# Attention and FFN in one kernel: softmax denominators spread by DMA, a projection bank shared, and 28 more score units on VectorE

## The chip, the cores and the metric

The kernel runs on one core of a Trainium2 chip. The metric is device time in microseconds (us) of one execution; the time before is 755.69 us, the median of three runs (754.64 to 756.87). Engines: TensorE (PE; its weight loads are PEld), VectorE (DVE), ScalarE (ACT), GpSimd (POOL) and SyncE (SP), whose queue issues nearly all DMAs.

## The reference

S = 2048 rows, D = 640, H = 32 query heads of Dh = 20 that share one key and one value head, F = 1536. All inputs are bf16.

```python
def _A_ref(x, wq, wk, wv, wo):
    q = (x @ wq).reshape(B, S, H, Dh).transpose(0, 2, 1, 3)
    k = x @ wk
    v = x @ wv
    scores = jnp.einsum("bhqd,bkd->bhqk", q, k) * (Dh ** -0.5)
    p = _softmax(scores, axis=-1)
    o = jnp.einsum("bhqk,bkd->bhqd", p, v)
    return o.transpose(0, 2, 1, 3).reshape(B, S, H * Dh) @ wo
def _B_ref(x, w1, b1, w2, b2):
    h = jnp.einsum("bsd,df->bsf", x, w1) + b1
    r = jnp.where(h > 0, h, 0)
    return jnp.einsum("bsf,fd->bsd", r * r, w2) + b2
xn = _layernorm(x, axis=-1)
return x + _A_ref(xn, A_wq, A_wk, A_wv, A_wo) + _B_ref(xn, B_w1, B_b1, B_w2, B_b2)
```

## The kernel before

**Blocks, tiles, units.** The queries are cut into 4 chunks of 512 rows and the heads into 8 groups of 4, which makes 32 blocks. A block needs the scores of its 4 heads against 16 tiles of 128 keys; a *unit* is one head against one tile (128 keys x 512 queries, one PSUM bank). Four units of a tile make one group of value products (PV), whose four heads stand in rows 0, 32, 64 and 96 of one PSUM bank. In the value operand, column 20 holds ones, so row 32h + 20 of the result is the softmax denominator of head h.

**Two ways to an exponential.** Most units go to ScalarE, which reads two or three banks at once and writes exp into `PT` (L790, `S_EXP`). The `QUOTA` list says how many of each block's 16 tiles go to VectorE instead: `[1, 3] + [4, 3, 4] * 9 + [4, 4, 4]`, 115 tiles or 460 units. There one instruction per unit turns scores into integers (`S_P1`, L875, result in `T8`), and four instructions per tile (`S_PH`, L901, result in `PB`) make four shifted copies whose bits are read as bf16 and whose weighted sum, made by four groups of PV products instead of one, approximates the exponential. A VectorE tile therefore costs four L875, four L901 and four PV groups.

**Banks.** Banks 0 to 2 and 3 to 5 are the two triples for scores. The third bank of each triple (2 is `XD`, 5 is `DB`) holds either the third unit of an exponential or one unit for VectorE. Bank 6 is `PVB` (the PV sum) and bank 7 `MB`, in which projections of queries, FFN rows and outputs (L521) are made one after the other (`S_MISC`).

**Who sets the order.** The program has a planner: while it is built, generators (`S_QK`, `S_D`, `S_PV`, `norm` and others) ask for instructions with modelled durations, and `Sched.run` writes one fixed list per engine from them. Each engine then executes its list in that order and waits on semaphores where a result is not there. `pos()` is the place in the ScalarE units, in blocks; `gates` say from which position a VectorE tile may start; the `U(at, ...)` list gives the position from which a projection may start. The planner counts 60 ns for an SP issue and a fixed landing time for each DMA. Requests marked `under` are GpSimd instructions that are put beneath a VectorE instruction that reads PSUM (`beneath`), after the last VectorE instruction marked `port`.

**Normalization.** When a block's PV sum is complete, `norm` transposes it out of PSUM in 32 x 32 squares (L987), which brings the denominators into columns, takes reciprocals of 128 x 16 values (L991), multiplies in two halves on GpSimd (L993) and transposes back into `OTn` (L1013), the operand of the output projection. The outputs of a chunk (`u_OUT`, L521 and L642) follow once its eight blocks are normalized; those of the last chunk are made in two parts, the first (`u_P1`) during the last blocks, the rest after the end of the scores. `out_tail` adds the residual from `x_sb`, which has stayed in SBUF since the start, and stores with a DMA on SP (L647).

**FFN.** `u_FFN` makes 12 rows of the hidden layer per chunk (L607), which GpSimd squares (L617); the `U` list spaces them half a block apart.

Of the kernel before, what the change touches and what calls it, by code (L numbers as in the profile page):

```python
# [14 lines left out]
HPG = 4  # L15
# [25 lines left out]
QUOTA = [1, 3] + [4, 3, 4] * 9 + [4, 4, 4]  # L41
RING = 20
NT8 = 3
NPB = 5
NQS = 4
EVP = 1
DLEAD = 0.45
DWAIT = 120.0
DALONE = 1500.0
DBEHIND = (1.5, 0.0)  # L50
QLATE = 0.15
PG, PAT = 4, 28.4

SEM_NS = 60.0
PE_WIN = 3420.0
PE_MISC = 9000.0
# [28 lines left out]
class Req:  # L85


    def __init__(self, alts, deps, prio, name="", mode=None, deadline=None, rows=None, after=0.0, cols=0.0, even=False, port=False, under=False):
        self.alts = alts if isinstance(alts, list) else [alts]
        self.deps, self.prio, self.name, self.mode = deps, prio, name, mode  # L90
        self.deadline, self.rows, self.after = deadline, rows, after
        self.cols, self.even, self.port, self.under = cols, even, port, under
# [7 lines left out]
class Sched:  # L100
# [17 lines left out]

    def room(self, t, c):
        tot = self.load(t) + c  # L120
        for s_, c_ in self.win:
            if tot <= PE_MISC:
                break
            if s_ > t - PE_WIN:
                tot -= c_
                t2 = s_ + PE_WIN
                t = max(t, t2)
        return t
# [19 lines left out]
    def run(self):  # L148
        while self.streams:
# [7 lines left out]
            cands = []  # L157
            for st in self.streams:
# [7 lines left out]
                if deps is None or rr.under:  # L166
                    continue
                t0 = max([d.done + SEM_NS for d in deps] + [rr.after])
                best = None
                for k, (eng, dur, lat, ins) in enumerate(rr.alts):  # L170
# [3 lines left out]
                    if rr.even:  # L174
                        est = self.room(est, rr.cols)
# [4 lines left out]
                cands.append((best[1], best[2], rr, deps, best[3], best[4], st))  # L180
            if not cands:
                raise RuntimeError("stuck at %.0f: %s" % (self.now, [s[2] for s in self.streams]))
# [70 lines left out]
    def resolve(self, newsem):  # L253
# [37 lines left out]
        for e in self.ENG:  # L291
            n = 0
            for op in self.lists[e]:
                if op.dma is not None:
                    op.sig, op.sem, op.amt, op.val = True, newsem("d_" + op.dma), 16, 16
                elif op.sig:
                    n += 1
                    op.sem, op.amt, op.val = sems[e], 1, n

    def emit(self, eng, e):  # L300
        for op in self.lists[eng]:
# [7 lines left out]
            for f in op.ins:  # L309
                ins = f(e)  # L310
            if op.sig and op.ins:
# [6 lines left out]
def bass_parallel_sum__grouped_kv_mqa__dense_activation_squared_relu__prompt_kernel(nc, A_x, A_wq, A_wk, A_wv, A_wo, B_x, B_w1, B_b1, B_w2, B_b2, out):  # L318
    es = ExitStack()
    with es:  # L320
# [3 lines left out]
        x_sb = sb("x_sb", [128, ST, D], BF16)  # L324
# [21 lines left out]
        PB = sb("PB", [128, NPB, HPG, 512], I16)  # L346
        Tn = sb("Tn", [128, 2, 512], F32)
        rd = sb("rd", [128, 2, 16], F32)
        T2 = sb("T2", [128, 2, 512], BF16)
# [37 lines left out]
        def dma(eng, name, fn, deps, land):  # L387
            def gen():
                op = yield Req((eng, 60.0 if eng == "sp" else 500.0, land, [fn]), deps, 0, name)
# [134 lines left out]
        def groups(gl, n, b_, deps, p, name, m=32, gdeps=None):  # L524
            v = None
            for k, (L, R) in enumerate(gl):
# [3 lines left out]
                elif gdeps is not None:  # L530
                    dd = dd + gdeps[k]
                v = yield Req(("pe", PE512 if n > 400 else PE320, (PE512 if n > 400 else PE320) + PELAT, col4(L, R, n, b_, k == 0, k == len(gl) - 1, m)),
                              dd, p, name, mode="col", cols=512.0 if n > 400 else 320.0, even=p >= 3)
# [89 lines left out]
        olast = {}  # L623

# [14 lines left out]
        def out_tail(v, st, hh, in1, b_, extra=()):  # L639
# [5 lines left out]
            olast[(st, hh)] = w  # L645
            if (st, 1 - hh) in olast:
# [8 lines left out]
        def u_OUT(qc, st, hh, b_):  # L655
# [7 lines left out]
            yield from out_tail(v, st, hh, x_sb[:, st, cs], b_)  # L663

        def u_P1(st, hh, gs, b_):
# [5 lines left out]
            v = yield Req(("dve", 450.0, 491.0, [lambda e: e.tensor_tensor(out=part[:, st % 4, cs], in0=ps[:, b_, 0:320], in1=x_sb[:, st, cs], op=ALU.add)]), [v], EVP, f"PE1_{st}_{hh}")  # L671
            done[f"PP{st}_{hh}"] = v
            bank[b_].last = [v]
# [7 lines left out]
        def u_FULL(st, hh, b_):  # L681
# [4 lines left out]
            yield from out_tail(v, st, hh, x_sb[:, st, cs], b_)  # L686
# [51 lines left out]
        def S_QK():  # L738
            k = 0
            slot = 0  # L740
            while apos[0] < len(aunits):
# [4 lines left out]
                n = 2 if busy[b3] or ("DBfree" if b3 == DB else "XDfree") not in done or d_behind() > DBEHIND[k % 2] else 3  # L746
# [64 lines left out]
        mbusy = [0]  # L811
        gates = [b + m / float(QUOTA[b]) - DLEAD for b, m, t in dtiles] + [float(NBLK)]

        def d_behind():
            p = pos()
            want = sum(4.0 * min(1.0, max(0.0, (p - gates[n]) / (gates[n + 1] - gates[n]))) for n in range(len(dtiles)))
            return want - nd[0]
        phq = []

        def S_D():  # L820
            todo = list(enumerate(dtiles))
            opened = []
            while todo or opened:
# [10 lines left out]
                def poll():  # L834
                    fb = [x for x in (DB, XD) if not busy[x] and (open3[x] or "QKend" in done) and bank[x].last is not None]
                    if not fb:
# [48 lines left out]

        def S_PH():
            for want in range(len(dtiles)):
# [5 lines left out]
                op = None  # L893
                for j in range(NPH):
                    k = (n * NPH + j) % NPB

                    def deps():
                        if pbres[k].last is None:
                            return None
                        return [acc[-1]] + pbres[k].last  # L900
                    op = yield Req(("dve", 600.0, 640.0, [lambda e, j=j, k=k, s=s: e.tensor_scalar(out=PB[:, k, :, :], in0=T8[:, s, :, :], scalar1=PH_D[j], scalar2=0.5,  # L901
                                                                                             op0=ALU.add, op1=ALU.mult)]), deps, 4, "PH", port=True)
                    pbres[k].last = None
                    pv_items[b].append(("D", t, (j, k), op))
                t8res[s].last = [op]
# [5 lines left out]
        def S_FILL():  # L911
# [4 lines left out]
            while "QKend" not in done:  # L916
                def poll():
# [7 lines left out]
                    if not pv_open[0]:  # L925
                        fb = [x for x in (MB, DB) if not (busy[DB] or not open3[DB] if x == DB else mbusy[0]) and "DBfree" in done and max(o.done for o in bank[x].last) + SEM_NS <= t + 40.0]
# [57 lines left out]
        def norm(b, pv):  # L984
            qc, g = divmod(b, G)
            a = b % 2
            v = yield Req(("dve", 700.0, 717.0, [lambda e: e.transpose(out=Tn[:, a, :], in_=ps[:, PVB, :])]), (lambda: get(*([f"NB{b - 2}"] if b >= 2 else [])) and [pv] + get(f"NB{b - 2}") if b >= 2 else [pv]), 0, f"N1_{b}")  # L987
            bank[PVB].last = [v]
            if b == NBLK - 1:
                done["PVend"] = True  # L990
            w = yield Req(("dve", 160.0, 234.0, [lambda e: e.reciprocal(out=rd[:, a, :], in_=Tn[:, a, DH:512:32])]), [v], 1.5, f"N2_{b}")  # L991
            def n3(e, c0, c1):
                return e.tensor_tensor(out=T2[:, a, 32 * c0:32 * c1].rearrange("p (c d) -> p c d", d=32), in0=Tn[:, a, 32 * c0:32 * c1].rearrange("p (c d) -> p c d", d=32),  # L993
                                       in1=rd[:, a, c0:c1].rearrange("p (c o) -> p c o", o=1).to_broadcast([128, c1 - c0, 32]), op=ALU.mult)
            if b == NBLK - 1:
                w = yield Req(("dve", 650.0, 688.0, [lambda e: n3(e, 0, 16)]), [w], 1.5, f"N3_{b}", port=True)
            else:
                r = w
                w = yield Req(("pool", 540.0, 600.0, [lambda e: n3(e, 0, 8)]), [r], 0, f"N3_{b}", under=True)
                w = yield Req(("pool", 540.0, 600.0, [lambda e: n3(e, 8, 16)]), [r], 0, f"N3_{b}", under=True)  # L1000

            def deps():
                dd = [w]
                if b < 2:
                    dd += done["junk"]
                if qc >= 2:
                    names = [f"O{qc - 2}_{st}_{hh}" for st in range(4 * qc - 8, 4 * qc - 4) for hh in range(2)]
                    o = get(*names)
                    if o is None:
                        return None  # L1010
                    dd += o
                return dd
            w = yield Req(("dve", 690.0, 707.0, [lambda e: e.transpose(out=OTn[:, qc % 2, g, :], in_=T2[:, a, :])]), deps, 1.5, f"N4_{b}")  # L1013
# [165 lines left out]
```

## Time and profile before

| | us |
|---|---|
| median of three runs | 755.69 |
| the profiled execution's own time | 755.73 |
| its span, first to last instruction | 753.9 |
| first exponential starts / last ends | 16.2 / 743.5 |
| TensorE's granted clock over the run | 0.998 of full |

The span is made of a ramp of about 25 us in which x is loaded, normalized and transposed, a long stretch of scores, and a tail from 743.5 us on with the last block's normalization and the last projections. The waits of VectorE's instructions:

```profile
DVE T L875 <- PE ps L728: 23.0, 30, 2.4
DVE hT_tmp L607 <- PE ps L521: 3.8, 4, 1.9
DVE w_sb L671 <- PE ps L521: 3.2, 2, 1.9
DVE qT L579 <- PE ps L521: 2.0, 2, 1.8
```

Each line names the waiting instruction and what it waited for, then the total in us, the number of times and the longest wait. A long total is only of weight where the engine that waits is needed at that time.

### The profile page before, as it was taken

How to read it: one execution, taken by the hardware profiler on the slowest of the kernel's cores; microseconds unless marked ns; L12 is line 12 of the kernel's file. 1: busy time of each engine (PE TensorE's matmuls, PEld its weight loads, DVE VectorE, ACT ScalarE, POOL GpSimd, SP SyncE). 2: the span in 40 equal slices, each digit the busy share in tenths (PEclk: the TensorE clock that was granted, in tenths of full speed). 3: DMA queues.
4: the chain of work that ended last, by engine and by line, in shares of the span. 5: the costliest groups of instructions: out<-in, count | busy, mean ns of one | idle time of the engine just before them, and what ended most of it. 6: DMA issues, size and time to landing. Idle time of an engine off the chain costs nothing.

```text
span 753.9 us, 22837 instructions
## 1 busy us (share of the span) xinstructions
PE 725.3 (96%) x10243; PEld 234.6 (31%) x10243; DVE 702.5 (93%) x1222; ACT 734.0 (97%) x756; POOL 113.1 (15%) x200
## 2 busy tenths in 40 slices
PE   8999999999999999999999999999999999999996
PEld 3422222222233333332223333333223333333333
DVE  6789999999998998999999989989999998899995
ACT  5999999999999999999999999999999999999994
POOL 4321111111011111012221001101222100000000
PEclk9999999999999999999999999999999999999999
DMA  8600000000000000000000000000000000000001
GB/s 257 184 2 1 2 2 2 1 2 2 1 3 10 2 10 2 10 2 10 2 2 3 10 3 10 2 10 10 2 2 2 5 7 11 11 11 2 3 2 37
DMA packets 9412, 12.33 MB, mean 16 GB/s; under 512 B 1761, under 2 KB 8674, under 8 KB 9314
## 3 DMA queue, kind: packets, MB, share of 16 engines
q1 hardware_dynamic: 8002, 10.82, 4.5%
q8 instruction: 80, 1.31, 0.8%
q10 hardware_dynamic: 1312, 0.05, 0.1%
q14 instruction: 18, 0.15, 0.1%
HBM read 8.25 MB, written 2.62 MB: 14 GB/s over the span
## 4 chain that ended last, share of the span: by engine, by line
ACT 84%; PE 15%; DVE 1%; issue 0%; POOL 0%; DVEq 0%; POOLq 0%
ACT PT L790 84%; PE ps L521 4%; PE ps L967 4%; PE ps L728 4%; PE ps L440 1%; DVE out_sb L642 0%; PE ps L915 0%; DVE kT L545 0%; PE ps L510 0%; DVE Tn L987 0%; DVE OTn L1013 0%; DVE T L993 0%; DVE xnT L505 0%; POOL hT_tmp L422 0%; DVEq L320 0%
## 5 line engine op out<-in xcount | busy, mean ns | idle before, releaser
L790 ACT ACTIVATE PT<-ps 128x1024 bf16<-128x1024 f32 (+2 forms) x733 | 725.8, 1182 | 1.6 <-PE ps L728 1.5
L875 DVE TENSOR_SCALAR T<-ps 128x512 uint16<-128x512 f32 x460 | 302.9, 678 | 24.1 <-PE ps L728 23.0
L728 PE MATMUL ps<-qT,kT 20*128 20x512 bf16 x2048 | 287.6, 384 | 19.9 <-ACT PT L790 16.2
L901 DVE TENSOR_SCALAR PB<-T 128x2048 int16<-128x2048 uint16 x460 | 299.8, 685 | 0.9
L967 PE MATMUL ps<-PB,vp 128*32 128x512 bf16 x1840 | 166.7, 382 | 1.1 <-DVE PB L901 0.6
L728 PEld LDWEIGHTS ps<-qT,kT 20*128 20x128 bf16 x2048 | 71.3, 91 | 283.4 <-ACT PT L790 271.7
L967 PE MATMUL ps<-PT,vx 128*32 128x512 bf16 x1588 | 157.7, 389 | 0.0
L617 POOL TENSOR_TENSOR big<-hT_tmp 128x256 bf16<-128x256 bf16 x96 | 58.4, 614 | 306.4 <-DVE PB L901 154.7
L521 PE MATMUL ps<-w_sb,big 128*32 128x320 bf16 x1536 | 85.2, 301 | 0.0
L993 POOL TENSOR_TENSOR T<-Tn,rd 128x256 bf16<-128x256 f32 x62 | 37.9, 617 | 285.5 <-DVE PB L901 212.8
L521 PE MATMUL ps<-xnT,w_sb 128*32 128x512 bf16 x960 | 77.7, 382 | 0.3 <-DVE out_sb L642 0.2
L967 PEld LDWEIGHTS ps<-PT,vx 128*32 128x32 bf16 x1588 | 40.5, 93 | 82.8 <-issue 81.5
L967 PEld LDWEIGHTS ps<-PB,vp 128*32 128x32 bf16 x1840 | 44.8, 95 | 45.3 <-issue 16.3
L521 PE MATMUL ps<-wo_pad,OTn 128*32 128x320 bf16 x1024 | 54.2, 301 | 0.8 <-DVE OTn L1013 0.8
L521 PE MATMUL ps<-xnT,wq_sb 128*20 128x512 bf16 x640 | 51.2, 380 | 0.0
L521 PEld LDWEIGHTS ps<-w_sb,big 128*32 128x32 bf16 x1536 | 36.7, 96 | 28.1 <-issue 15.4
L607 DVE TENSOR_SCALAR hT_tmp<-ps,b1col 128x512 bf16<-128x512 f32 x48 | 35.5, 739 | 4.3 <-PE ps L521 3.8
L521 PEld LDWEIGHTS ps<-wo_pad,OTn 128*32 128x32 bf16 x1024 | 24.6, 96 | 18.5 <-issue 7.4
L521 PEld LDWEIGHTS ps<-xnT,w_sb 128*32 128x32 bf16 x960 | 21.8, 95 | 22.0 <-issue 10.6
L912 PE MATMUL ps<-kT,zeros 128*32 128x512 bf16 x276 | 24.9, 381 | 0.0
L987 DVE STREAM_TRANSPOSE Tn<-ps 128x512 f32<-128x512 f32 x32 | 22.7, 710 | 1.0 <-PE ps L967 0.9
L579 DVE TENSOR_SCALAR qT<-ps 128x512 bf16<-128x512 f32 x31 | 21.2, 685 | 2.5 <-PE ps L521 2.0
(56 smaller groups left out, 169.7 us busy)
## 6 DMA issues: line engine op xcount, KB each, us to landing
w_sb<-in_B_w_dram SPq DMA_DIRECT2D x2, 1920.0 KB, 11.8
out_dram<-out_sb SPq DMA_DIRECT2D x16, 160.0 KB, 1.8
x_sb<-in_A_x_dram SPq DMA_DIRECT2D x3, 640.0 KB, 8.9
wq_sb<-in_A_wq_dram SPq DMA_DIRECT2D x1, 800.0 KB, 6.4
wo_pad<-in_A_wo_dram SPq DMA_DIRECT2D x4, 200.0 KB
x_sb<-in_A_x_dram SPq DMA_DIRECT2D x2, 320.0 KB, 4.0
wk_c<-in_A_wk_dram ACTq DMA_DIRECT2D x1, 25.0 KB, 3.8
wv_c<-in_A_wv_dram ACTq DMA_DIRECT2D x1, 25.0 KB, 4.6
```

Of the source, the lines that this page charges most:

```text
L521: return lambda e: e.matmul(ps[32 * j:32 * j + m, b_, 0:n], Lj, R, start=first, stop=last, tile_position=(0, 32 * j))
L579: alts = [("dve", 620.0, 660.0, [lambda e: e.tensor_scalar(out=dst, in0=ps[:, b_, :], scalar1=QSCALE, scalar2=None, op0=ALU.mult)])]
L607: v = yield Req(("dve", 690.0, 750.0, [lambda e: e.tensor_scalar(out=hT_tmp[:, k, :], in0=ps[:, b_, :], scalar1=b1col[:, f:f + 1], scalar2 ...
L617: w = yield Req(("pool", 540.0, 600.0, [lambda e, hs=hs: e.tensor_tensor(out=h2T[:, qc % 2, f, hs], in0=hT_tmp[:, k, hs], in1=hT_tmp[:, k, ...
L728: ins.append(lambda e, i=i, b=b, t=t, h=h: e.matmul(ps[:, b0 + i, :], kT[32 * h:32 * h + DH, t * 128:(t + 1) * 128], qT[32 * h:32 * h + DH ...
L790: op = yield Req(("act", d_, d_ + 100.0, [lambda e, slot=slot, n=n, b0=b0: e.activation(out=PT[:, slot:slot + n, :], in_=ps[:, b0:b0 + n, ...
L875: op = yield Req(("dve", 600.0, 660.0, [lambda e, s=s, h=h, bk=bk: e.tensor_scalar(out=T8[:, s, h, :], in0=ps[:, bk, :], scalar1=OFFS, sca ...
L901: op = yield Req(("dve", 600.0, 640.0, [lambda e, j=j, k=k, s=s: e.tensor_scalar(out=PB[:, k, :, :], in0=T8[:, s, :, :], scalar1=PH_D[j], ...
L912: fill = [(lambda e, h=h: e.matmul(ps[32 * h:32 * h + 32, PVB, :], zeros32[:, :], kT[:, 0:512], start=False, stop=False, tile_position=(0, ...
L967: ins = [(lambda e, h=h, first=first, last=last: e.matmul(ps[32 * h:32 * h + 32, PVB, :], lhs, rhs[h], start=first, stop=last, tile_positi ...
L987: v = yield Req(("dve", 700.0, 717.0, [lambda e: e.transpose(out=Tn[:, a, :], in_=ps[:, PVB, :])]), (lambda: get(*([f"NB{b - 2}"] if b >= ...
L993: return e.tensor_tensor(out=T2[:, a, 32 * c0:32 * c1].rearrange("p (c d) -> p c d", d=32), in0=Tn[:, a, 32 * c0:32 * c1].rearrange("p (c ...
```

## The change

1. **Quota.** `[1, 3] + [4] * 29 + [2]`: 122 tiles, 488 units on VectorE, 1560 on ScalarE. `T8` has four buffers instead of three and `PB` six instead of five; `PB` takes the next free buffer instead of a fixed one.
2. **Denominators.** Except for the last block, both transposes go. A copy brings the PV sum to SBUF; four DMAs spread the four denominator rows over 32 partitions each, VectorE takes the reciprocals, four DMAs bring them back into rows, and four DMAs broadcast each row over its head's 32 partitions. GpSimd multiplies, straight into `OTn`. The last block keeps the old way (`norm_last`).
3. **Banks.** VectorE units may also use the projection bank `MB` while no projection is due and at most two units are open; the choice between two and three units for an exponential follows whether a VectorE unit is due and none is in flight.
4. **FFN rows.** They may start from block 0.8, 4.0, 12.2 and 20.2 for the four chunks, 0.2 blocks apart.
5. **Space.** `PB` lies where `x_sb` was; the residual is loaded again from DRAM, 16 DMAs of one row tile each into `xres`.
6. **The planner.** `under` requests may also be placed while VectorE is free for their length; the pacing of projections (`even`, `room`) goes. An option to share L901's work with GpSimd is added and off (`SHARE = False`).

```diff
-QUOTA = [1, 3] + [4, 3, 4] * 9 + [4, 4, 4]
+QUOTA = [1,3]+[4]*29+[2]
-NT8 = 3
-NPB = 5
+NT8 = 4
+NPB = 6
+SHARE = False
-DBEHIND = (1.5, 0.0)
+FAT = (0.8, 4.0, 12.2, 20.2)
+FSTEP = 0.2
+MBD = 2
+MBSLACK = .02
+MBEND = 30.0
+GIVE = 2
+OUTM = (1,1)
...
+                if rr.under:
+                    eng, dur, lat, ins = rr.alts[0]
+                    est = max(self.free[eng], t0, self.port, self.free["dve"])
+                    below.append((est, dur, rr, deps + ([self.last_port] if self.last_port is not None else []), 0, eng, st))
+                    continue
...
+            idle = min([c[0] for c in cands if c[5] == "dve"] + [1e12])
+            cands += [c for c in below if c[0] + c[1] <= idle + 50.0]
...
-        x_sb = sb("x_sb", [128, ST, D], BF16)
+        pbx = sb("pbx", [128, NPB * HPG * 512], I16)
+        PB = pbx[:, :].rearrange("p (k h n) -> p k h n", k=NPB, h=HPG)
+        x_sb = pbx[:, 0:ST * D].bitcast(BF16).rearrange("p (st d) -> p st d", st=ST)
+        xres = sb("xres", [128, 4, D], BF16)
...
+        def x_again(st):
+            yield Until(lambda: pos() >= min(8 * (st // 4) + 7.0, PAT - 1.0) and (st < 4 or ((st - 4, 0) in xuse and (st - 4, 1) in xuse)))
+            dma("sp", f"xr{st}", lambda e: e.dma_start(xres[:, st % 4, :], xv[:, st, :]), [xuse[(st - 4, hh)] for hh in range(2)] if st >= 4 else [], 2500.0)
...
-                n = 2 if busy[b3] or ("DBfree" if b3 == DB else "XDfree") not in done or d_behind() > DBEHIND[k % 2] else 3
+                n = 2 if busy[b3] or ("DBfree" if b3 == DB else "XDfree") not in done or wants() and nd[0] - nd[1] < OUTM[k % 2] else 3
...
-                    if not fb:
+                    if not busy[MB] and not mbusy[0] and misc_slack() and nd[0] - nd[1] < MBD:
+                        fb.append(MB)
+                    if not fb or nd[0] - nd[1] >= GIVE:
                         return None
...
-            w = yield Req(("dve", 690.0, 707.0, [lambda e: e.transpose(out=OTn[:, qc % 2, g, :], in_=T2[:, a, :])]), deps, 1.5, f"N4_{b}")
+            v = yield Req(("dve", 640.0, 700.0, [lambda e: e.tensor_copy(out=Tn[:, a, :], in_=ps[:, PVB, :])]), (lambda: None if old() is None else [pv] + old()), 0, f"N1_{b}")
+            bank[PVB].last = [v]
+            dma("sp", f"da{b}", [(lambda e, h=h: e.dma_start(dn[32 * h:32 * h + 32, a, :], Tn[32 * h + DH:32 * h + DH + 1, a, :].rearrange("p (r c) -> p r c", c=16))) for h in range(HPG)], [v], 2300.0)
+            yield Until(lambda: have(f"da{b}"))
+            w = yield Req(("dve", 90.0, 160.0, [lambda e: e.reciprocal(out=rd[:, a, :], in_=dn[:, a, :])]), [done[f"da{b}"]], 1.5, f"N2_{b}")
+            dma("sp", f"db{b}", [(lambda e, h=h: e.dma_start(Rr[32 * h:32 * h + 1, :].rearrange("p (r c) -> p r c", c=16), rd[32 * h:32 * h + 32, a, :])) for h in range(HPG)],
+                [w] + ([] if b < 1 else [done[f"dc{b - 1}"]]), 2300.0)
+            yield Until(lambda: have(f"db{b}"))
+            dma("sp", f"dc{b}", [(lambda e, h=h: e.dma_start(Rb[32 * h:32 * h + 32, a, :], Rr[32 * h:32 * h + 1, :].rearrange("p (o n) -> p o n", o=1).to_broadcast([1, 32, 512]))) for h in range(HPG)],
+                [done[f"db{b}"]] + old(), 2600.0)
+            yield Until(lambda: have(f"dc{b}"))
+            w = []
+            for i in range(2):
+                c = slice(256 * i, 256 * i + 256)
+                w.append((yield Req(("pool", 540.0, 600.0, [lambda e, c=c: e.tensor_tensor(out=OTn[:, qc % 2, g, c], in0=Tn[:, a, c], in1=Rb[:, a, c], op=ALU.mult)]),
+                                    (lambda: None if free() is None else [done[f"dc{b}"]] + free()), 0, f"N3_{b}", under=True)))
+            done[f"NB{b}"] = w[-1]
...
-                at = 1.0 + (FT * qc + f) * 0.5
+                at = FAT[qc] + f * FSTEP
```

## The prediction

> **What bounds the kernel now.** I read the engines' busy shares first, then the chain that ended last, then the busy times of the stretch between the ramp and the tail (25 to 735 us), then who waited for whom, and last the timeline of ScalarE and VectorE.
>
> ```profile
> PE 725.3 (96%) x10243; PEld 234.6 (31%) x10243; DVE 702.5 (93%) x1222; ACT 734.0 (97%) x756; POOL 113.1 (15%) x200
> ACT 84%; PE 15%; DVE 1%; issue 0%; POOL 0%; DVEq 0%; POOLq 0%
> ```
> ```profile
> 25.00:735.00 710.00, 690.67 (x9739) 218.27 (x9731) 673.47 (x1143) 709.30 (x720) 103.41 (x173) 1.00 0.02 6
> ```
> The numbers after the length are PE, PEld, DVE, ACT and POOL. ScalarE is busy in 709.3 of 710 us: its exponentials (L790) set the pace. VectorE follows with 673.5, 95%; it has 36.5 us left.
>
> ```profile
> L790 ACT ACTIVATE PT<-ps 128x1024 bf16<-128x1024 f32 x609 | 583.1, 1110 | 1.6 <-PE ps L728 1.5
> L875 DVE TENSOR_SCALAR T<-ps 128x512 uint16<-128x512 f32 x460 | 302.9, 678 | 24.1 <-PE ps L728 23.0
> L901 DVE TENSOR_SCALAR PB<-T 128x2048 int16<-128x2048 uint16 x460 | 299.8, 685 | 0.9
> L790 ACT ACTIVATE PT<-ps 128x1536 bf16<-128x1536 f32 x123 | 187.6, 1542 | 0.0
> L987 DVE STREAM_TRANSPOSE Tn<-ps 128x512 f32<-128x512 f32 x32 | 22.7, 710 | 1.0 <-PE ps L967 0.9
> L1013 DVE STREAM_TRANSPOSE OTn<-T 128x512 bf16<-128x512 bf16 x32 | 22.5, 702 | 0.2
> L993 POOL TENSOR_TENSOR T<-Tn,rd 128x256 bf16<-128x256 f32 x62 | 37.9, 617 | 285.5 <-DVE PB L901 212.8
> ```
> 460 score units go through VectorE (L875 once each, L901 four times per tile of four units), 609 x 2 + 123 x 3 + 1 = 1588 through ScalarE. A duration here includes a drain that the next instruction overlaps, so costs must be taken from start to start.
>
> ```profile
> 31.02 1.07 ACT L790 ACTIVATE PT<-ps 128x1024 bf16<-128x1024 f32 x1
> 32.75 27.61 ACT L790 ACTIVATE PT<-ps 128x1024 bf16<-128x1024 f32 x30 [0.65 <-PE ps L728]
> ```
> ```profile
> 308.21 1.89 DVE L901 TENSOR_SCALAR PB<-T 128x2048 int16<-128x2048 uint16 x3
> 316.20 1.28 DVE L875 TENSOR_SCALAR T<-ps 128x512 uint16<-128x512 f32 x2
> 319.29 0.70 DVE L987 STREAM_TRANSPOSE Tn<-ps 128x512 f32<-128x512 f32 x1
> 319.92 0.65 DVE L875 TENSOR_SCALAR T<-ps 128x512 uint16<-128x512 f32 x1
> ```
> Two-unit exponentials start every (27.61 - 1.07) / 29 = 0.915 us. All 733 take 725.8 us, so a three-unit one costs (725.8 - 610 x 0.915) / 123 = 1.36: 0.458 and 0.454 us per unit. L901 costs (1.89 - 0.68) / 2 = 0.605, L875 1.28 - 0.68 = 0.60, a transpose 0.63.
>
> **The change part by part.** *Units moved.* The quotas sum to 115 tiles before and 122 after: 28 units more on VectorE, 1560 on ScalarE. ScalarE loses 28 x 0.457 (725.8 / 1588) = 12.8 us, and its need in the stretch is 709.3 - 12.8 = 696.5. How exponentials are grouped is worth nothing: three of two units cost 2.75, two of three 2.72. So the projection bank lent to score units (MB as third bank for a VectorE unit) and the new rule for two or three units act only by feeding VectorE; I cost them at nothing, covered by TensorE, whose score loads waited 271.7 us for ScalarE. Bounds: if feeding VectorE becomes harder, its idle stays (second rival); if easier, the 23.0 us that L875 sat waiting for scores go to zero. VectorE gains 28 x 0.60 + 28 x 0.605 = 33.7 us.
>
> *Denominators.* For 31 of 32 blocks the second transpose (L1013) goes: -31 x 0.63 = -19.5. The first (L987) becomes a copy of the same PSUM tile; the nearest rows are L875 at 0.60 and the transpose itself at 0.63, so -0.9 to 0; I take -0.5. The reciprocal keeps 128 x 16 elements: 0. VectorE's need is 673.5 + 33.7 - 19.5 - 0.5 = 687.2, or 98.7% of the 696.5 that ScalarE then needs. It has 9.3 us to lose before it is the bound, and 710 - 687.2 = 22.8 us before the kernel is slower than now.
>
> *The DMA relay.* Each block puts three groups of four DMAs on SP's queue (row out, reciprocal's result back, broadcast over 32 partitions): 372 issues. No such transfer, inside SBUF and in 64-byte pieces, is in the trace; the nearest rows are the output stores.
>
> ```profile
> out_dram<-out_sb SPq DMA_DIRECT2D x16, 160.0 KB, 1.8
> ```
> Their issue occupies SP's queue 0.332 us (0.383 at most); two loads at the start took 0.95 together; landing takes 1.8 (2.5 at most). A group of four so lands 3 x 0.332 + 1.8 = 2.8 us after its release. From below: half the landing for 8 KB instead of 160, 1.9; from above 3 x 0.475 + 2.5 = 3.9. The planner counts 60 ns for an issue and 2300 ns for the first two groups, 2600 for the broadcast. VectorE executes in the written order, and the new wait is the reciprocal's, written about 2.42 us after the first copy ends, plus on average half an instruction (0.3): 2.7. Behind it stand the L901 and L875 instructions, and for these wait TensorE's products with PB. So it is late by 2.8 + 0.1 for waking - 2.7 = 0.2 on average: 31 x 0.2 = 6 us of VectorE; from below 0, from above 31 x 1.2 = 37. I take 6, as a small transfer is nearer to the lower row than to the upper.
>
> The Trainium skill's DMA: Bandwidth & Descriptors, section Anatomy of one DMA, puts a fixed cost of about 2.0 us on a DMA, mostly the write's receipt (a fit for the other, software path). By it the group would land at 3.0, the lateness be 0.4, and the sum some 6 us higher; the stores' 1.8 for 160 KB disagrees, and I keep the rows.
>
> *GpSimd's product.* The two halves (0.617 each, 62 in all) now wait for the third group. Second and third group together land in 2 x 2.9 = 5.8 against some 5.1 in the written order, so they come some 0.7 late, more if the broadcast (256 KB) takes longer than a store. The trace shows what late means: GpSimd waits 212.8 us for L901 by the planner's order, so that each half runs under an instruction that reads PSUM, and L901 never exceeds 0.729 against a median of 0.684. A late half may run into L901 instead. From below 0, from above 62 x 0.617 = 38 us; I take one half in three colliding for 0.3: 6 us.
>
> *The rest.* Seven more tiles give TensorE 7 x 3 more groups of four products at about 0.21 (two groups 0.61, one 0.40): 4.4 us, covered by 69 filler groups (276 / 4) that can go. Sixteen reloads of x (160 KB each) take SP 16 x 0.33 and are due a block, some 22 us, ahead of use; x's old place holds PB, which is first written at 43.5 us, after x is normalized. FFN rows come in denser runs: 48 x 0.66 of VectorE stays the same in sum. The first projection of a chunk's output waits for the eighth block's norm, which now ends some 6 us later; I put three times 0.5 us on it (0 to 3 x 3), since lower-priority work stands there. The pacing of projections that is dropped could not act: it allowed 9000 columns in 3420 ns, and one group of 512 takes 0.21 us, 8300 in that time. In the last block two tiles fewer end on VectorE; the end of its last L901 (744.6 us) was what the last product waited for, 1.1 us after ScalarE: -0.5.
>
> **Sum.** ScalarE alone: 753.9 - 12.8 = 741.1. VectorE's need with relay and collisions, 687.2 + 6 + 6 = 699.2, is 2.7 above 696.5, and of its former 13 us of waits for other things than scores (36.5 - 23) I let a fifth stay on the path, 2.6. With 1.5 and -0.5 from the last part: 741.1 + 2.7 + 2.6 + 1.0 = 747.4 of span. The runs' median of 755.69 lies 1.8 above the span (the profiled run itself took 755.73); so 749.2, rounded 749. Own range: 743 (nothing lost: 742.9) to 755.
>
> **Rivals.** *ScalarE stays the only bound* (chance 0.2): VectorE's waits shrink as work is always there, and the relay lands in time. For it: all but 1.6 us of ScalarE's stretch is gapless today, and L875's 23.0 us of waiting are spread over 30 places with VectorE underfed. Against: 98.7%. Time 743 to 744.
>
> *VectorE's relay wait becomes the bound* (0.36, the other side). Place: the reciprocal behind the first group, and GpSimd's late halves. It decides from 22.8 us lost, 0.74 per block. With a group landing at 3.9, lateness 1.2, it is 37 us, and with a third of the collisions' bound (13) 50: 710 becomes 737, the time 783; with half of that (25) 758; I put this case at 765. The Trainium skill's SBUF: State Buffer, section Who interferes with whom, says that a VectorE instruction in a two-port mode and a GpSimd instruction hold one port pair exclusively and the other blocks: by it collisions cost the whole overlap, which makes this rival dearer; the trace shows the ordering that avoids it and no block.
>
> *VectorE's old idle does not shrink* (0.06): 687.2 + 36.5 = 723.7, 13.7 above 710: 769. For it: L875 waits for scores in every 100 us of the run. Against: VectorE had less work than time, so some idle had to be somewhere.
>
> **How the numbers follow.** My case has 0.38, of which 0.04 lies above 753.4. A change under 0.3% (753.4 to 758.0) can't be told from none here. Faster: 0.2 + 0.34 = 0.54. Same: 0.04 from my case and 0.06 from the relay rival's mild end, 0.10. Slower: 0.30 + 0.06 = 0.36. The range goes from 742 (a tail shorter by another microsecond) to 771; I leave some 0.15 beyond 771 and 0.04 below.
>
> **What would show it.** Right: L790 with 1560 units and some 713 us; VectorE above 97% between ramp and tail; reciprocal preceded by idle with a DMA as releaser, 0 to 0.5 us a block; L901's maximum near 0.73. Wrong: ScalarE idle for 15 us or more, waiting for TensorE, which waits for VectorE (the relay); L901 instructions of 0.9 us or more (collisions); L875 still waiting over 20 us for scores.

## The result and the profile after

The changed kernel takes 835.94 us (median of four runs, 826.92 to 839.26) against 755.79: a ratio of 1.104, 95% interval 1.095 to 1.113. It is slower by 80 us, 65 us beyond the upper end of the range. Where a run below took over 1.5% longer than the fastest of its kernel, at a lower clock, the medians still count it and the ratios with their intervals don't; "without slower runs" names the median of the others.

The lines that answer to those of before, from the page of the profiled execution (span 824.8 us, time 826.92):

```profile
PE 779.1 (94%) x10255; PEld 243.1 (29%) x10255; DVE 720.5 (87%) x1246; ACT 738.2 (90%) x765; POOL 133.8 (16%) x200
PEclk9999999799988999999789999999589999959999
DVE 46%; PE 28%; DMA 11%; SPq 7%; ACT 4%; issue 3%; POOL 1%; DVEq 0%; POOLq 0%
L811 ACT ACTIVATE PT<-ps 128x1024 bf16<-128x1024 f32 (+1 forms) x742 | 730.0, 1090 | 68.7 <-PE ps L749 62.2
L939 DVE TENSOR_SCALAR pbx<-T 128x2048 int16<-128x2048 uint16 x488 | 323.1, 698 | 0.1
L1084 POOL TENSOR_TENSOR OTn<-Tn,Rb 128x256 bf16<-128x256 f32 x62 | 55.5, 916 | 502.1 <-DMA Rb<-Rr 459.9
L1074 DVE RECIPROCAL rd<-dn 128x16 f32<-128x16 f32 x31 | 7.8, 253 | 32.3 <-DMA dn<-Tn 32.3
Rb<-Rr SPq DMA_DIRECT2D x124, 64.0 KB, 5.8
dn<-Tn SPq DMA_DIRECT2D x124, 2.0 KB, 1.7
```

L811 is the exponential (L790 before), L939 the four shifted copies (L901 before), L749 the scores, L1074 the reciprocal and L1084 GpSimd's product. ScalarE is no longer gapless: it sat idle 68.7 us before exponentials (1.6 before), nearly always for scores. DMA and SP's queue have 18% of the chain that ended last, where they had nothing. The reciprocal waited 32.3 us in all for the first group of DMAs. And the row PEclk has dips that the kernel before does not have in its score stretch: the clock granted to TensorE averages 0.948 against 0.998. The trace's clock record shows eight half-speed periods of 3.4 to 23.9 us within the score stretch, 85.3 us together.

How two of them begin, in the timeline of the changed kernel (start, duration, engine, line, instruction; in brackets the idle time before it and what ended that). The first two lines stand before the period of 6.8 us that begins at 426.0 us, the others before the longest, from 579.6 us on:

```profile
424.30 0.25 DVE L1074 RECIPROCAL rd<-dn 128x16 f32<-128x16 f32 x1 [2.73 <-DMA dn<-Tn]
425.15 0.40 PE L1035 MATMUL ps<-pbx,vp 128*32 128x512 bf16 x4 [2.03 <-DVE pbx L939]
569.31 3.14 SPq L1078 DMA_DIRECT2D Rb<-Rr  x4
571.02 0.74 DVE L619 TENSOR_SCALAR hT_tmp<-ps,b1col 128x512 bf16<-128x512 f32 x1
578.83 1.41 POOL L1084 TENSOR_TENSOR OTn<-Tn,Rb 128x256 bf16<-128x256 f32 x2 [10.02 <-DMA Rb<-Rr]
580.19 2.33 POOL L629 TENSOR_TENSOR big<-hT_tmp 128x256 bf16<-128x256 bf16 x4
580.91 0.75 DVE L619 TENSOR_SCALAR hT_tmp<-ps,b1col 128x512 bf16<-128x512 f32 x1 [6.15 <-POOL big L629]
581.72 0.61 PE L533 MATMUL ps<-xnT,wq_sb 128*20 128x512 bf16 x4 [5.58 <-DVE hT_tmp L619]
582.90 1.02 ACT L811 ACTIVATE PT<-ps 128x1024 bf16<-128x1024 f32 x1 [5.88 <-PE ps L749]
```
The longest in windows (length, busy time of PE, PEld, DVE, ACT and POOL, granted clock, DMA share, GB/s):
```profile
560.00:570.00 10.00, 9.98 (x134) 2.69 (x126) 8.80 (x16) 10.00 (x12) 0.61 (x1) 1.00 0.03 4
580.00:590.00 10.00, 8.28 (x58) 1.59 (x62) 6.38 (x11) 4.73 (x5) 3.13 (x6) 0.50 0.02 5
590.00:600.00 10.00, 10.00 (x76) 1.75 (x68) 5.43 (x11) 6.62 (x7) 0.00 (x0) 0.50 0.02 2
610.00:620.00 10.00, 9.70 (x124) 2.62 (x116) 10.00 (x16) 9.78 (x11) 4.60 (x6) 1.00 0.10 7
```

At 424 us the reciprocal waits 2.73 us for the first group; the L939 behind it comes late, and TensorE stands idle for 2.03. At 579 us the product on GpSimd waits for the broadcast. Behind it in GpSimd's list stand four squares of FFN rows (L629); the next FFN row on VectorE (L619) needs the two buffers that these free and waits 6.15 us; TensorE's next projection needs the bank that this row reads and waits 5.58; and ScalarE gets no scores for 5.88 us. From 579.6 us on, 2 us before this stop ends, the clock is at half for 23.9 us: TensorE is busy throughout 590 to 600 us but gives ScalarE work for 6.6 of 10. By the same views, four of the eight periods follow a reciprocal's wait of 1.5 to 2.7 us and four a late product, three of these over FFN rows and one (at 245.1 us) over the output projection, for which TensorE waited 3.3 us. Within the eight periods ScalarE is busy 51.2 of 85.3 us: 34.2 of its idle time lie there, though in all but some 2 of the 85.3 us TensorE is working.

### The profile page after: what moved, and what is told of

Read it like the earlier page. It is cut to its first block, busy times and chain, and to the rows that moved or that the text cites. A ratio compares the mean times of both kernels' runs of the same rounds, so it can differ in the third digit from the quotient of the medians.

```text
span 824.8 us, 23339 instructions
## 1 busy us (share of the span) xinstructions
PE 779.1 (94%) x10255; PEld 243.1 (29%) x10255; DVE 720.5 (87%) x1246; ACT 738.2 (90%) x765; POOL 133.8 (16%) x200
## 4 chain that ended last, share of the span: by engine, by line
DVE 46%; PE 28%; DMA 11%; SPq 7%; ACT 4%; issue 3%; POOL 1%; DVEq 0%; POOLq 0%
DVE pbx L939 20%; DVE T L903 19%; PE ps L533 9%; PE ps L1035 8%; PE ps L749 8%; DMA dn<-Tn 6%; SPq L1072 6%; DMA Rb<-Rr 4%; ACT PT L811 4%; DVE Tn L1070 2%; DVE hT_tmp L619 2%; DVE qT L591 1%; DMA Rr<-rd 1%; DVE out_sb L661 1%; PE ps L452 1%
## 5 line engine op out<-in xcount | busy, mean ns | idle before, releaser
L811 ACT ACTIVATE PT<-ps 128x1024 bf16<-128x1024 f32 (+1 forms) x742 | 730.0, 1090 | 68.7 <-PE ps L749 62.2
L903 DVE TENSOR_SCALAR T<-ps 128x512 uint16<-128x512 f32 x488 | 318.2, 680 | 21.7 <-PE ps L749 21.6
L939 DVE TENSOR_SCALAR pbx<-T 128x2048 int16<-128x2048 uint16 x488 | 323.1, 698 | 0.1
L749 PE MATMUL ps<-qT,kT 20*128 20x512 bf16 x2048 | 310.1, 398 | 11.6 <-ACT PT L811 5.4
L1035 PE MATMUL ps<-pbx,vp 128*32 128x512 bf16 x1952 | 191.9, 403 | 16.2 <-DVE pbx L939 15.0
L749 PEld LDWEIGHTS ps<-qT,kT 20*128 20x128 bf16 x2048 | 76.1, 91 | 291.5 <-ACT PT L811 198.6
L1084 POOL TENSOR_TENSOR OTn<-Tn,Rb 128x256 bf16<-128x256 f32 x62 | 55.5, 916 | 502.1 <-DMA Rb<-Rr 459.9
L533 PE MATMUL ps<-xnT,w_sb 128*32 128x512 bf16 x960 | 86.5, 413 | 3.4 <-DVE hT_tmp L619 3.1
L629 POOL TENSOR_TENSOR big<-hT_tmp 128x256 bf16<-128x256 bf16 x96 | 61.5, 655 | 149.9 <-DVE hT_tmp L619 76.2
L1035 PEld LDWEIGHTS ps<-pbx,vp 128*32 128x32 bf16 x1952 | 49.6, 96 | 83.3 <-DVE pbx L939 51.7
L619 DVE TENSOR_SCALAR hT_tmp<-ps,b1col 128x512 bf16<-128x512 f32 x48 | 35.7, 744 | 11.7 <-POOL big L629 8.7
L1074 DVE RECIPROCAL rd<-dn 128x16 f32<-128x16 f32 x31 | 7.8, 253 | 32.3 <-DMA dn<-Tn 32.3
L1070 DVE COPY Tn<-ps 128x512 f32<-128x512 f32 x31 | 21.1, 681 | 3.6 <-PE ps L1035 3.5
```

The source lines that it names most:

```text
L533: return lambda e: e.matmul(ps[32 * j:32 * j + m, b_, 0:n], Lj, R, start=first, stop=last, tile_position=(0, 32 * j))
L619: v = yield Req(("dve", 690.0, 750.0, [lambda e: e.tensor_scalar(out=hT_tmp[:, k, :], in0=ps[:, b_, :], scalar1=b1col[:, f:f + 1], scalar2 ...
L629: w = yield Req(("pool", 540.0, 600.0, [lambda e, hs=hs: e.tensor_tensor(out=h2T[:, qc % 2, f, hs], in0=hT_tmp[:, k, hs], in1=hT_tmp[:, k, ...
L749: ins.append(lambda e, i=i, b=b, t=t, h=h: e.matmul(ps[:, b0 + i, :], kT[32 * h:32 * h + DH, t * 128:(t + 1) * 128], qT[32 * h:32 * h + DH ...
L811: op = yield Req(("act", d_, d_ + 100.0, [lambda e, slot=slot, n=n, b0=b0: e.activation(out=PT[:, slot:slot + n, :], in_=ps[:, b0:b0 + n, ...
L903: op = yield Req(("dve", 600.0, 660.0, [lambda e, s=s, h=h, bk=bk: e.tensor_scalar(out=T8[:, s, h, :], in0=ps[:, bk, :], scalar1=OFFS, sca ...
```

## The experiments

**First round: is it the relay, VectorE's fill, or the rest of the change?** The theory after the result: the written order expects the transfers too early, and what stands behind them takes the clock down. Rivals: VectorE is too full whatever the relay does; or the denser FFN rows and the lent bank starve the scores.

*e1: only the planner's numbers for the relay:* the cost of an issue, the landing of the first group (the second has the same edit) and that of the broadcast.
```diff
-... 60.0 * len(fl) if eng == "sp" ...
+... (600.0 * len(fl) if len(fl) > 1 else 60.0) if eng == "sp" ...
...
-... [v], 2300.0)
+... [v], 3700.0)
...
-... + old(), 2600.0)
+... + old(), 8000.0)
```


> The changed kernel in which only the planner's numbers for the relay are set to what the trace of after shows: 600 ns per SP issue instead of 60, landing of a group of four 3.7 us instead of 2.3 for the first two groups, 8.0 us instead of 2.6 for the broadcast. Relay theory (the written order expects the transfers too early; GpSimd and VectorE stand still behind them, TensorE behind these, and its clock falls): the order now leaves the time, waits on the first group under 5 us in all, granted clock 0.99 or more, 743 to 753 us. Rival (VectorE is simply too full at 98.7%, whatever the relay does): still 765 or more, VectorE near 100% busy. Rival (denser FFN rows or the lent bank starve the scores and drop the clock): 800 or more, clock still about 0.95.


Measured 764.27 us, ratio 1.011 (1.008 to 1.013), clock 1.0. No instruction of the work was changed, only the order; 72 of the 80 us are gone. But it missed its range by 11 us, and the reciprocal still waited 8.0 us where under 5 were expected: see e12 and e14.

*e3: the old quotas.*
```diff
-QUOTA = [1,3]+[4]*29+[2]
+QUOTA = [1, 3] + [4, 3, 4] * 9 + [4, 4, 4]
```


> The changed kernel with the quotas of before (460 units on VectorE), all else as changed. Relay theory: the late transfers still stop GpSimd and VectorE, the clock still falls below 0.97; VectorE's 30 us of relief absorb a part only: 785 to 830 us. Rival (VectorE too full): the cause is gone, 753 to 760 us at a clock of 0.99 or more.


Measured 858.97 us, ratio 1.134 (1.131 to 1.138). It isn't the quota; the relief on VectorE absorbed nothing, and this mix of late transfers came out worse than the changed kernel, above what the theory had given it; why it is worse stays open.

*e5: no transfers.* The three groups are left out; reciprocal and product read constants.
```diff
-            dma("sp", f"da{b}", ...)
-            dma("sp", f"db{b}", ...)
-            dma("sp", f"dc{b}", ...)
...
+            done["fake"] = yield ms(Rb[:, :, :], 1.0, 1000.0, "rb1")
```


> The changed kernel without the twelve transfers per block: reciprocals and products read constants that are written once at the start, so the denominators of all blocks but the last are left out; the instructions on VectorE and GpSimd and their number stay. Relay theory: no wait, clock 0.99 or more, 743 to 752 us. Rival (VectorE too full): 765 or more. Rival (FFN rows, lent bank): 800 or more with a clock of about 0.95.


Measured 752.09 us, ratio 0.995 (0.994 to 0.997): just at the end of the range. So VectorE's fill, FFN rows and banks together cost nothing against before, and this kernel, whose relay takes no time, is some 4 us faster than before. That is no limit for other orders: e9 and e10 come out lower still.

*e2: both transposes in every block*, the rest as changed.
```diff
-            if b == NBLK - 1:
+            if True:
                 yield from norm_last(b, pv, old, free)
```
(`norm_last` then splits its product over GpSimd as before.)


> The changed kernel with the normalization of before (two transposes) in every block, and the new quotas, banks, FFN rows and space. Relay theory: no DMA waits and a clock of 0.99 or more; VectorE needs 687.2 + 20.0 = 707 us between ramp and tail, more than ScalarE's 696.5, so VectorE bounds: 760 to 772 us. Rival (FFN rows, lent bank): 800 or more with a clock of about 0.95.


Measured 765.36 us, ratio 1.012 (1.011 to 1.014): as expected for a VectorE that needs about 20 us more. It was busy 699.5 of 710 us between 25 and 735, and ScalarE idle 20.8 us before exponentials. Taking the transposes away is thus worth 13 us in this order (765.36 to 752.09), if what replaces them costs nothing.

**Second round: which transfer, and what a stall costs.**

*e6 and e7: true times for the broadcast and second group only, or for the first group only* (the diff of e1, in part).


> The changed kernel with true times (600 ns an issue, 3.7 us the second group, 8.0 us the broadcast) for the second and third group only; the first group is still written as landing after 2.3 us. If GpSimd's late products (the broadcast) start most of the stalls: 768 to 785 us, the reciprocal still waits 25 to 35 us in all. If the reciprocal's wait on VectorE starts them: 800 us or more, clock 0.97 or less.


Measured 849.27 us (842.8 without slower runs), ratio 1.116 (1.106 to 1.125), clock 0.919 in the profiled execution; the reciprocal waited 37.2 us.


> The counterpart: true times for the first group only, the broadcast still written as landing after 2.6 us. If the broadcast starts most of the stalls: 800 us or more at a clock of 0.97 or less, the reciprocal's waits under 8 us. If the reciprocal's wait does: 765 to 785.


Measured 780.26 us (778.7 without slower runs), ratio 1.030 (1.024 to 1.036), clock 0.984; reciprocal's waits 10.6 us, GpSimd's product still waiting for the broadcast at all 31 blocks. The reciprocal in e6, then in e7:

```profile
L1074 DVE RECIPROCAL rd<-dn 128x16 f32<-128x16 f32 x31 | 7.8, 253 | 37.2 <-DMA dn<-Tn 37.2
L1074 DVE RECIPROCAL rd<-dn 128x16 f32<-128x16 f32 x31 | 7.7, 248 | 10.6 <-DMA dn<-Tn 10.6
```

So the small wait is the dear one: the reciprocal's, 0 to 2.7 us in each of 31 blocks of the changed kernel and 1.04 on average, on the engine that has least to spare. In e6 all eight half-speed periods of the score stretch follow a reciprocal's wait of 1.5 to 2.4 us. The late broadcast, though longer (some 9.4 us), costs 778.7 - 764.1 = 15 us over e1 without slower runs. It reaches the other engines only where FFN rows or an output projection stand behind it, by the traces: e7 has one half-speed period, of 23.9 us, and it begins while an output projection waits 3.13 us for the product.

*e8: the kernel before, with eight stops of TensorE.*
```diff
+        def stall(i, at, n):
+            yield Until(lambda: pos() >= at)
+            prev = sc.lists["pe"][-1]
+            for k in range(n):
+                op = yield Req(("sp", 1.0, 1.0, [lambda e: e.dma_start(probe[1:2, :], probe[0:1, :])]), [prev], -9, f"pr{i}_{k}")
+                op.dma = f"pr{i}_{k}"
+                prev = op
+            yield (lambda: Req(("pe", 1.0, 1.0, []), [prev], -9, "prw", mode=sc.mode))
+        for i, (at, n) in enumerate([(3.5, 1), (6.5, 1), (9.5, 2), (12.5, 2), (15.5, 3), (18.5, 3), (21.5, 4), (24.5, 4)]):
+            sc.spawn(stall(i, at, n), "stall")
```


> The kernel before, in which TensorE is stopped eight times by a chain of one, one, two, two, three, three, four and four 64-byte DMAs that the planner doesn't count; nothing else is changed. With some 1.8 us a link TensorE stands still for 36 us in all. If a stall costs only itself less the 0.9 us that ScalarE has ahead: 36 - 7 = 29 us at most, 785 us, clock 0.99 or more. If a stall also halves the clock for some microseconds, as after the stalls of the changed kernel: half-clock periods of 3 to 20 us behind the longer stalls, clock 0.96 to 0.98, and 790 to 815 us.


Measured 807.02 us, ratio 1.068 (1.064 to 1.071), clock 0.960. From its trace: the product that ends each stop, for two, three, three and four links (the bracket is the stop, the idle time between TensorE's products; their ends are modelled), and the windows after the two stops of three links:

```profile
316.75 0.72 PE L523 MATMUL ps<-w_sb,big 128*32 128x320 bf16 x8 [2.76 <-DMA probe<-probe]
393.94 0.61 PE L523 MATMUL ps<-xnT,w_sb 128*32 128x512 bf16 x4 [4.40 <-DMA probe<-probe]
469.19 0.61 PE L730 MATMUL ps<-qT,kT 20*128 20x512 bf16 x3 [4.46 <-DMA probe<-probe]
625.69 1.04 PE L523 MATMUL ps<-xnT,wq_sb 128*20 128x512 bf16 x8 [6.08 <-DMA probe<-probe]
```
```profile
394.00:401.00 7.00, 7.00 (x56) 1.38 (x56) 3.48 (x5) 3.50 (x3) 1.84 (x3) 0.51 0.00 0
469.00:479.00 10.00, 9.81 (x78) 2.09 (x78) 5.22 (x8) 5.55 (x5) 1.02 (x2) 0.50 0.01 2
```

The eight stops and the half-speed periods that came with them, from the clock record (four of these begin 0.1 to 3.0 us before the stop ends, and the second 3.4 of the first row 11 us after its stop):

| links | stop, us | half speed, us |
|---|---|---|
| 1 | 1.50, 1.38 | 3.4 and again 3.4; none |
| 2 | 2.85, 2.76 | 3.4; 13.7 |
| 3 | 4.40, 4.46 | 6.8; 10.2 |
| 4 | 5.87, 6.08 | 13.7; 6.8 |

The stops add up to 29.3 us, the span grew by 805.8 - 753.9 = 51.9. Between 25 and 790 us ScalarE is idle for 49.4 us: 20.9 of these lie in the stops, and 23.2 in the 54.2 us in which TensorE works at half speed outside them. That is 0.43 us lost per microsecond at half speed. Applied to the changed kernel's 85.3 us it makes 37 of its 71 us more in span, near the 34.2 us of ScalarE's idle time found inside such periods. This share is an estimate; that a stop of TensorE brings the clock down is shown, since here nothing else was changed.

**Third round: can the relay be made to work?**

*e9: one DMA a group,* four heads in one access pattern; landing written as 2.5, 2.5 and 8.0 us; GpSimd's product in three slices.
```diff
-[(lambda e, h=h: e.dma_start(dn[32 * h:32 * h + 32, a, :], Tn[32 * h + DH:32 * h + DH + 1, a, :].rearrange("p (r c) -> p r c", c=16))) for h in range(HPG)]
+[lambda e: e.dma_start(dn[:, a, :], Tn[DH:128:32, a, :].rearrange("p (r c) -> p r c", c=16))]
...
-            for i in range(2):
+            for i in range(3):
```


> The changed kernel with one DMA for each group in place of four (all four heads in one access pattern), written as landing after 2.5, 2.5 and 8.0 us, and GpSimd's product in three slices of 500 ns in place of two of 540. Relay theory: fewer issues shorten a group by 3 x 0.6 us, the short slices fit under an instruction that reads PSUM; clock 0.99 or more, 750 to 760 us, L939's mean back to some 0.685. Rival (what is left in e1_true_times over the kernel without a relay is VectorE's fill, not collisions or waits): 762 to 768.


Measured 749.94 us, ratio 0.993 (0.991 to 0.995), clock 1.0: 0.7% faster than before, and just below its range. Its page:

```profile
L811 ACT ACTIVATE PT<-ps 128x1024 bf16<-128x1024 f32 (+1 forms) x743 | 716.3, 1122 | 4.8 <-PE ps L1035 3.0
L1084 POOL TENSOR_TENSOR OTn<-Tn,Rb 128x171 bf16<-128x171 f32 (+1 forms) x93 | 49.9, 550 | 398.5 <-DVE pbx L939 383.5
L1074 DVE RECIPROCAL rd<-dn 128x16 f32<-128x16 f32 x31 | 7.7, 247 | 0.0
```
The reciprocal waits for nothing, and GpSimd's product is held back by L939, as the order wants it, and no longer by the DMA (459.9 us of waits there in the changed kernel, 15.0 here).

*e11: one DMA a group and nothing else;* landing times and slices as changed.


> The changed kernel with one DMA for each group in place of four and nothing else: the planner's landing times (2.3, 2.3, 2.6 us) and the two slices of 540 ns stay as changed. If the mis-sized term was the four issues of a group (3 x 0.6 us ahead of the last landing), the reciprocal waits under 8 us in all, the clock is 0.97 or more, 755 to 785 us (late broadcasts remain). If the landing itself was too late: 800 us or more.


Measured 764.75 us (758.88 to 772.48; 761.7 without slower runs), ratio 1.008 (1.004 to 1.011). With three issues fewer the first group is there at its written place: the reciprocal's idle time in its profile is 0.0. Most of the 80 us hung on these three issues a group, for which the order had left no time. The broadcast is still late: its product starts 7.0 us after the issue, against 2.6 written, and in the profiled execution, the slowest of the six, one half-speed period of 34.1 us follows a product that held FFN rows back.

*e12 and e14: four DMAs a group again, with three slices, and then the broadcast written as 10.8 us.*


> e1_true_times (four DMAs a group) with GpSimd's product in three slices in place of two. If collisions of the long halves (0.86 us on average) with L939 are what e1 loses: 752 to 757 us, L939's mean at 0.687 or less. If it is the four issues and what they delay: 761 to 766.


Measured 764.92 us, ratio 1.015 (1.009 to 1.021): the slices alone change nothing against e1.


> e12_three_slices (four DMAs a group) with the broadcast written as landing after 10.8 us in place of 8.0; its trace and that of e1 show GpSimd's product starting 9.4 us or later after the first issue, so 8.0 was still too early. If the late product and its collisions are what is left of the loss: the product waits for L939 by the written order and no longer for the transfer, L939's longest under 1.05 us, 748 to 754 us. If four issues cost something else (the first group's wait, SP's queue): 758 or more.


Measured 755.11 us (752.71 to 762.61), ratio 1.003 (0.999 to 1.006). In e12 a product started 9.4 us or later after the first issue, so 8.0 had been too early; with 10.8 the longest L939 falls from 1.098 to 0.725 us. Ten of the 15 us between e12 and e9 went with this one number. The median lies 1 us above the range; 4.1 us of waits of the reciprocal remain, and what else is left of the 5 us stays open.

*e13: e9 with the old quotas.*


> e9_one_dma_a_group with the quotas of before. If the relay by itself gives nothing and only lets VectorE take units (28 units are worth 12.8 us of ScalarE's work): ScalarE bounds again, 752 to 757 us, VectorE with 25 us more idle than in e9. If the relay or the lent bank saves time in itself: 750 or less.


Measured 755.94 us, ratio 1.002 (1.000 to 1.004), ScalarE idle 1.6 us before exponentials, VectorE's score instructions idle 34.0. A relay that works, with the banks and the FFN rows of the change, gives nothing by itself: it makes room on VectorE, and the gain is the units that fill it.

*e10: e9 with the FFN rows spread,* the outputs closer together, one tile more on VectorE in the last block, and GpSimd's slices written as 530 ns in place of 500. VectorE was busy 4.0 of 20 us from 720 to 740 us in e9.
```diff
-QUOTA = [1,3]+[4]*29+[2]
-FAT = (0.8, 4.0, 12.2, 20.2)
-FSTEP = 0.2
-OSTEP = 0.5
+QUOTA = [1,3]+[4]*29+[3]
+FAT = (0.8, 4.5, 12.5, 18.5)
+FSTEP = 0.35
+OSTEP = 0.35
```


> e9_one_dma_a_group with the FFN rows 0.35 blocks apart (from block 0.8, 4.5, 12.5, 18.5) in place of 0.2, outputs 0.35 apart in place of 0.5, three tiles of the last block on VectorE in place of two, and GpSimd's slices written as 530 ns. VectorE stood nearly idle for the last 30 us of e9; if the bunched FFN rows push VectorE's units late and their absence leaves it empty at the end, an even spread gains 3 to 6 us: 744 to 748. If ScalarE and the tail set the time whatever the rows do: 749 to 751.


Measured 745.95 us, ratio 0.987 (0.985 to 0.989): the best version, 10 us faster than before. It fits bunched rows that had cost some of what the units bring; as four things changed together, the share of the rows alone is not shown.

```profile
span 743.6 us, 23200 instructions
L811 ACT ACTIVATE PT<-ps 128x1024 bf16<-128x1024 f32 (+1 forms) x739 | 714.8, 1121 | 2.8 <-PE ps L749 1.5
```

## Why the prediction was wrong

*Units moved.* The forecast took 12.8 us off ScalarE. Between e13 and e9, which differ in the quotas alone, the exponentials' busy time falls from 726.3 to 716.3 us and the time by 6.0 us. Right in sign; about half of the 12.8 reached the end, as ScalarE had gaps again (4.8 us against 1.6 in e13) and the tail behind the last exponential was 1.6 us longer.

*Denominators.* VectorE was to need 13.7 us more than before. In e9, where it hardly waits, its busy time over the whole run is 708.7 against 702.5: 6.2 more. That it would have room was right (e5, e9); why it needs less than forecast no run separates.

*The DMA relay: the step that failed.* "A group of four so lands 3 x 0.332 + 1.8 = 2.8 us after its release." The landing was well chosen: 1.7. The issue was mis-sized: the row taken from the stores says 0.332, but an issue inside SBUF with 32 pieces takes 0.50 us at least and 0.59 in the median, and four take 2.41 from first to last. From the timelines of SP's queue, the four issues of a group in the changed kernel and the one of e9:

```profile
224.57 2.41 SPq L1072 DMA_DIRECT2D dn<-Tn  x4
230.76 0.52 SPq L1072 DMA_DIRECT2D dn<-Tn  x1
```
So the group lands at about 3.6, the lateness is 1.04 us (32.3 / 31) in place of 0.2, and the term 32.3 us in place of 6, close to the upper bound of 37 that I had worked out and set aside, because the transfer is small. It is small; its issue isn't. The Trainium skill's 2.0 us for a DMA (DMA: Bandwidth & Descriptors, Anatomy of one DMA) would have been 0.3 too long for the landing.

*GpSimd's product.* The second and third group were to land in 5.8 us. The second does in 3.6; the broadcast alone takes 9.3 to 10.6 from first issue to product, 9.4 in the median (the longest from 211.44 to 222.02 us in the changed kernel's timeline). For "0.7 late" read 3.6 + 9.4 - 5.1 = 7.9 by the same sum. The 256 KB were priced like a store of 160; the load from one partition, read 32 times, has no row in the profile before, and the forecast gave its landing no upper bound. Collisions came, too: the longest L939 is 1.220 us against 0.729 before, and 0.728 in e10. In sum they are what the forecast gave them and not the 13 of the rival: L939's mean of 0.698 less its median of 0.683, times 488, is 7 us, against 6. All 20 that took over 0.85 us overlap a GpSimd instruction, which agrees with what the Trainium skill's SBUF: State Buffer, section Who interferes with whom, says of the shared port pair.

*What was behind the wait.* For the late product I named the output projection, with 1.5 us; it did wait, once, for 3.3. The squares of the FFN rows stand behind the product in the same queue, and behind these VectorE, which waited 8.7 us for them in all; this chain, seen at 569 to 583 us, was missing from the sum.

*The clock.* The forecast and all its rivals priced a wait at its own length. TensorE's granted clock of 0.998 stood in the table of the kernel before and was taken for granted. This is the largest missing term, some 37 us by the estimate from e8. With it, and with 32.3, 3.3 and 8.7 us for the three waits above, the forecast's sum of 747.4 becomes 821 against a span of 824.8; that, too, is an estimate, as such waits can overlap. The rival "VectorE's relay wait becomes the bound" had the right place and point of decision (more than 22.8 us lost) and the wrong price: 765, or 783 at worst, where 836 came. The Trainium skill's TensorE: Matmul & The Clock Gate, section What's actually happening, describes it: the clock goes to half after an idle window of about 3.4 us, and the windows run free. The lengths here, 3.4 to 23.9 us in steps of 3.41, agree, and so do the starts, which lie whole steps apart. The idle time does not: a stop of 1.50 us in e8 was enough once, and so, at 389 to 391 us of the changed kernel, were 0.41 and 0.93 us in close succession. So stops far shorter than 3.4 us can be enough, and no safe length is shown.

*The signs.* All three signs of being wrong came: ScalarE idle 68.7 us, L939 of 1.220 us, and score units on VectorE (L903) still waiting 21.6 us for scores. The last was the sign of the rival "VectorE's old idle does not shrink", but that rival is not the cause: in e9 the same units wait 4.9 us.

## What to carry to other kernels

In an order that is fixed when the program is built, a transfer that lands later than its place stops the engine with least slack, and everything behind it; price the issues of a group as well as its landing, and write the place from a measured landing. Merging small DMAs into one access pattern can be worth as much as such a reordering: here three issues fewer per group brought 836 us to 762, truer times in the planner to 764 (e1, both without slower runs) and to 755 (e14), and both together to 750 (e9). A stall of TensorE should be priced at its length and the half-speed time after it.

## What the runs showed of the hardware

An issue on SP's queue of a transfer inside SBUF with 32 pieces took 0.50 us at least and 0.59 in the median, against 0.33 for a store of 160 KB, and one of all four heads (128 pieces) took no more: 0.52 to 0.56. Four broadcasts of one row to 32 partitions each need 9.3 to 10.6 us from first issue to use; as one DMA the same 256 KB need 7.0 to 7.8 (e11). In the probe a stop of TensorE of 1.50 us was followed by half speed for 3.4 us, one of 1.38 us by none; with stops of 2.8 us and more it came each of six times. In e1 idle times of 0.92 and 1.11 us were followed by none, while in the changed kernel 0.41 and 0.93 us in close succession were.
